# Eight PSUM banks as one ring in a linear-attention and mixture-of-experts kernel, in place of four kinds of tiles with two banks each

## The chip, the cores and the metric

The kernel runs on one core of one Trainium2 chip. The metric is the device time of one execution in microseconds (us); the median of three runs is given.

## The reference

Three blocks follow each other. A gated linear attention over 4 sequences of 768 tokens, 8 heads of 48; a gated feed-forward layer of 3072 tokens; and a mixture of 8 experts in which each token goes to the best two by noisy logits.

```python
state = alpha[:, :, t, :, None] * state + einsum('bhd,bhe->bhde', k[:, :, t], v[:, :, t])
y[:, :, t] = einsum('bhd,bhde->bhe', q[:, :, t], state)
...
x = ((x @ w1) * (x @ w2) @ w3) @ w_out          # 384 -> 1024 -> 1024 -> 384
...
noisy = x @ w_gate + log1p(exp(x @ w_noise)) * noise
# top 2 of 8 experts a token, softmax over the two
out[mask] += weight * (relu(x[mask] @ w1[e]) @ w2[e])   # 384 -> 1024 -> 384
```

## The kernel before

The work has two parts that overlap in time on the chip. The first part works through 8 groups of 384 tokens (3 chunks of 128 each). For a group, `prep_decay` and `prep_qk` turn alpha, q and k to feature-major with TensorE transposes in `to_dmajor` (L207) and scale them with scans and products on VectorE (L223, L225, L234). For each chunk j, `scores` makes the 128x128 products of k and q (L287) that VectorE masks (L294, L304), `ktok` turns k back (L316), `mix` makes the output from the state and the scores (L326, L337) and `state` updates the state (L356). `xturn` (L389) turns the output to feature-major in float16, in a high and a low part. Then comes the feed-forward layer. `wide` (L510 to L531) multiplies 384 tokens with one block of 128 columns of w1 or w2 in nine matmuls (L519 to L521); ScalarE copies the bank out (L523, tile ab), VectorE multiplies the two results (L527), ScalarE rounds to float16 (gh, L179) and VectorE makes the rest (gl, L181). `narrow` (L533 to L551) multiplies 128 tokens with the product of w3 and w_out, which the kernel makes itself once (`fuse_out_turn`, `fuse_out`, `fuse_turn`, `fuse_mul`, L457 to L493). A `narrow` has two halves of 12 matmuls on one bank; the second half needs the gl of the last `wide` blocks. `route` and `rank` choose the experts.

The second part goes through the experts: `turn` (L882) turns gathered tokens, `layer1` (L889 to L891) and `layer2` (L899 to L901) or `layer2t` (L913 to L915) multiply them, and `put` adds them to the output by indirect DMA.

The order of the work on TensorE is written out by hand. `att_units` gives the attention's units with costs, `mix_units` those of the feed-forward layer, and the loop at L1150 to L1170 takes units of the second list as long as their cost stays in a fixed relation to the attention's. TensorE runs them in just this order. The other engines' order, all waits and the tiles' places are set when the program is built, from the same code. `warm` (L1135) issues matmuls that nobody reads.

PSUM has eight banks of 128 x 512 float32 each. One pool, `ps` (L128), holds four kinds of tiles by name, with two banks each. A tile takes the bank of the tile before the last of its own kind, and its first matmul waits until that one's last reader is done.

| kind | taken by |
|---|---|
| tr | `to_dmajor`, `ktok`, `xturn`, `fuse_out_turn`, `fuse_turn`, `over_all`, `turn`, the end of `last_few` |
| sc | `scores` (two at a time), `layer1` for odd blocks |
| yu | `mix`, `state`, `scales_of`, `rank`, `layer2`, `layer2t`, `overflow_plan` |
| mm | `wide`, `narrow`, `fuse_out`, `fuse_mul`, `warm`, `layer1` for even blocks |

The program takes 738 of these tiles in all, the loop for overflowing tokens at the end included, which has no turn with this input. Most of them are written and read before the next one is taken. A bank of `narrow` or `fuse_mul` is held over both halves, with up to six others taken in between.

Of the kernel before, what the change touches and what calls it, by code (L numbers as in the profile page):

```python
# [8 lines left out]
F32 = mybir.dt.float32  # L9
# [11 lines left out]
P = 128  # L21
# [3 lines left out]
E = 8  # L25
# [37 lines left out]
T1 = 2  # L63
PGL = range(4)
NPC = 4
WE = 16
LAG = 3
WPOS = (14, 17, 17, 17, 17, 18, 18, 19, 20, 20, 20, 20)
# [15 lines left out]
def body(ctx, tc, q, k, v, alpha, mw1, mw2, mw3, mwo, wg, wn, noise, ew1, ew2, out, dbg=None):  # L84
# [40 lines left out]
    xp = ph1.enter_context(tc.tile_pool(name="xp", bufs=3))  # L125
    sp = ph1.enter_context(tc.tile_pool(name="sp", bufs=2))
    gp = ph1.enter_context(tc.tile_pool(name="gp", bufs=2))
    ps = ph1.enter_context(tc.tile_pool(name="ps1", bufs=2, space=PSUM))  # L128
    stg_ = ExitStack()
    stg = stg_.enter_context(tc.tile_pool(name="stg", bufs=2))  # L130

# [53 lines left out]
    def load(st):  # L185
# [11 lines left out]
        for c in range(TG):  # L197
# [3 lines left out]
            if st == 0:  # L201
                fetch(sum(w < len(loads) + c + 1 for w in WPOS), nc.sync)

    def to_dmajor(i, pr):
        tr = ps.tile([P, 3, P], F32, name="tr")
        for r in range(3):
            nc.tensor.transpose(tr[:, r, :], pads[i][:, r, 2 * pr:2 * pr + 2, :].rearrange("p h d -> p (h d)"),  # L207
                                ident)
        return tr
# [47 lines left out]
    def scales_of(st):  # L257

        if "ss" not in ST[st]:
            return  # L260
        V = nc.vector
        pm = ps.tile([P, 5], F32, name="yu")
        nc.tensor.matmul(pm, ones, ST[st].pop("ss"), start=True, stop=True)
        t = late.tile([P, 6], F32, name="sg")
        ti = t.bitcast(I32)
        SCL[st] = r = xp.tile([P, 4], F32, name="scl")
        V.tensor_copy(t[:, :2], pm[:, :2])
        V.tensor_reduce(t[:, 2:3], pm[:, 2:], AX.X, OP.add)
        V.tensor_scalar(ti[:, :3], ti[:, :3], 1, 0x7F800000, op0=OP.logical_shift_right, op1=OP.bitwise_and)
        V.tensor_scalar(ti[:, 3:], ti[:, :3], -1.0, float(192 << 23), op0=OP.mult, op1=OP.add)  # L270
        V.tensor_scalar(t[:, 3:], t[:, 3:], 2.0 ** 30, None, op0=OP.min)
        V.scalar_tensor_tensor(r[:, 0:1], t[:, 3:4], 2.0 ** 10, t[:, 4:5], op0=OP.mult, op1=OP.mult)
        V.tensor_scalar(r[:, 1:2], t[:, 5:6], 2.0 ** 12, None, op0=OP.mult)
        V.tensor_tensor(r[:, 2:3], r[:, 0:1], r[:, 1:2], OP.mult)
        V.tensor_scalar(r.bitcast(I32)[:, 3:4], r.bitcast(I32)[:, 2:3], -1.0, float(254 << 23), op0=OP.mult, op1=OP.add)
        CSL[st] = late.tile([P, P], F32, name="csl")
        V.tensor_scalar(CSL[st], causal, r[:, 0:1], None, op0=OP.mult)
# [3 lines left out]

    def scores(j):
        r, cols = cut(j)
        scs = [ps.tile([P, NP, P], F32, name="sc") for _ in range(2)]
        for h in range(H):
            rows = slice(64 * (h % 2), 64 * (h % 2) + D)
            nc.tensor.matmul(scs[h % 2][:, h // 2, :], r["Kt"][rows, h // 2, cols], r["Qt"][rows, h // 2, cols],  # L287
                             start=True, stop=True)
        SM[j] = []
        for s in range(2):  # L290
            if j // TG in SCL:
                sf = late.tile([P, NP, P], F32, name="sf")
                sm = late.tile([P, 2, NP, P], F16, name="sm16", bufs=4)
                nc.vector.tensor_tensor(sf, scs[s], CSL[j // TG][:, None, :].to_broadcast([P, NP, P]), OP.mult)  # L294
                split(sf, sm[:, 0], sm[:, 1], engine=nc.gpsimd)
                SM[j].append(sm)
                continue
            sm = ap_.tile([P, NP, P], F32, name="sm", bufs=3)
            if j in AFF:
                nc.scalar.activation(sm, scs[s], AF.Copy)  # L300
                nc.gpsimd.affine_select(out=sm, in_=sm, pattern=[[0, NP], [1, P]], compare_op=OP.is_ge, fill=0.0,
                                        base=0, channel_multiplier=-1)
            else:
                nc.vector.tensor_tensor(sm, scs[s], causal[:, None, :].to_broadcast([P, NP, P]), OP.mult)  # L304
            SM[j].append(sm)
        if j // TG in SCL:
            VH[j] = late.tile([P, 2, H, D], F16, name="vh")
            split(VT[j], VH[j][:, 0], VH[j][:, 1], SCL[j // TG][:, 1:2])

    def ktok(j):  # L310
        if j % NC == NC - 1:
            return
        r, cols = cut(j)
        kt = ps.tile([P, NP, P], F32, name="tr")
        for pr in range(NP):
            nc.tensor.transpose(kt[:, pr, :], r["Kt"][:, pr, cols], ident)  # L316
        KS[j] = ap_.tile([P, NP, P], F32, name="ks")
        nc.scalar.activation(KS[j], kt, AF.Copy)

    def mix(j):  # L320
        r, cols = cut(j)
        y = ps.tile([P, NP, 2 * D], F32, name="yu")
        n = 0
        if j % NC:
            for pr in range(NP):
# [22 lines left out]
    def state(j):  # L348
# [2 lines left out]
        if c == NC - 1:  # L351
            return
        ks, vt = KS.pop(j), VT[j]
        u = ps.tile([P, NP, 2 * D], F32, name="yu")
        for pr in range(NP):
            nc.tensor.matmul(u[:112, pr, :], ks[:, pr, :112], vt[:, 2 * pr:2 * pr + 2, :], start=True, stop=True)  # L356
        Z, Zn = Zs[j % 2], Zs[(j + 1) % 2]
# [25 lines left out]
    def xturn(j):  # L383
        ys = YS.pop(j)
        if j % TG == 0:
            XT[j // TG] = xp.tile([P, 2 * NK, G], F16, name="xT")
        xt = ps.tile([P, 2 * NK, P], F16, name="tr")
        for kk in range(2 * NK):
            nc.tensor.transpose(xt[:, kk, :], ys[:, kk // NK, kk % NK * P:(kk % NK + 1) * P], ident16)  # L389
        nc.scalar.activation(XT[j // TG][:, :, j % TG * P:(j % TG + 1) * P], xt, AF.Copy)  # L390
# [65 lines left out]

    def fuse_out_turn(f):  # L457
        wo = FS.pop(f)
        tr = ps.tile([P, NK, P], F32, name="tr")
        for kk in range(NK):  # L460
            nc.tensor.transpose(tr[:, kk, :], wo[:, kk * P:(kk + 1) * P], ident)
        FO[f] = stg.tile([P, NK, P], F32, name="woT")
        nc.scalar.activation(FO[f], tr, AF.Copy)

    def fuse_out(f):
        woT = FO.pop(f)
        pr = ps.tile([P, 2 * E], F32, name="mm")
        for kk in range(NK):
            nc.tensor.matmul(pr, woT[:, kk, :], wr[:, kk, :], start=kk == 0, stop=kk == NK - 1)
        split(pr, woh[:, f, DM:], wol[:, f, DM:], SW)  # L470

    def fuse_turn(f, hf):
        s = FS.pop((f, hf))
        th = stg.tile([P, 4, P], F16, name="w3h", bufs=3)
        tl = stg.tile([P, 4, P], F16, name="w3l", bufs=3)
        tr = ps.tile([P, 4, P], F32, name="tr")
        for j in range(4):
            nc.tensor.transpose(tr[:, j, :], s[:, j * P:(j + 1) * P], ident)
        split(tr, th, tl, SW)
        FT[f, hf] = (th, tl)  # L480

    def fuse_mul(f, hf):
        th, tl = FT.pop((f, hf))
        if hf == 0:
            FT[f] = ps.tile([P, W], F32, name="mm")
        pw = FT[f]
        for j in range(4):
            kk = 4 * hf + j
# [21 lines left out]
    def wide(g, f, i, c1=G):  # L510
# [3 lines left out]
        c0 = GS.get((g, f, i), 0)  # L514
        GS[g, f, i] = c1
        cs, n = slice(c0, c1), c1 - c0
        pm = ps.tile([P, G], F32, name="mm")[:, :n]
        for kk in range(NK):
            nc.tensor.matmul(pm, wab[i][0][:, kk, fs], xT[:, kk, cs], start=kk == 0, stop=False)  # L519
            nc.tensor.matmul(pm, wab[i][0][:, kk, fs], xT[:, NK + kk, cs], start=False, stop=False)  # L520
# [12 lines left out]
    def narrow(g, t, part):  # L533
        ts = slice(t * P, (t + 1) * P)
        if part == 0:
            X2[g, t] = ps.tile([P, W], F32, name="mm")
            if t == 0:
                X2[g] = sp.tile([P, TG, W], F32, name="x2", bufs=1)
                X2[g, "sq"] = sp.tile([P, 5, TG], F32, name="am")
# [98 lines left out]
    def rank(g):  # L638
# [1 line left out]
        V = nc.vector  # L640
        sh = [P, TG, E]
        M, oh, rr, md = RT.pop(g)
        pk = ps.tile([P, TG, E], F32, name="yu")
        nc.tensor.matmul(pk, before, M[:, 0], start=True, stop=False)
        nc.tensor.matmul(pk, ones, M[:, 1], start=False, stop=True)
        rk = sp.tile(sh, F32, name="rk")
# [1 line left out]
        if g == NG - 2:  # L648
            rb = sp.tile([P, E], BF, name="rb")
            V.tensor_copy(rb, R)  # L650
            pt = ps.tile([P, E], F32, name="yu")
            nc.tensor.matmul(pt, ones, rb, start=True, stop=True)
            V.tensor_scalar(skip, pt[:, :NFR], -1.0, float(G0), op0=OP.mult, op1=OP.add)
            V.tensor_scalar(skip, skip, 0.0, None, op0=OP.max)
# [174 lines left out]
    def weight_steps(src, e, n, m, hi, lo, sc):  # L829
# [19 lines left out]

        def over_all():  # L850

            s["pm"] = ps.tile([P, 1], F32, name="tr")
            nc.tensor.matmul(s["pm"], part, s["m"], start=True, stop=True)

        def scales():
# [21 lines left out]
        return xg  # L877

    def turn(xg, xT, t):
        pt = ps.tile([P, 2 * NK, P], F16, name="tr")  # L880
        for j in range(2 * NK):
            nc.tensor.transpose(pt[:, j, :], xg[:, j * P:(j + 1) * P], ident16)  # L882
        nc.scalar.activation(xT[:, :, t * P:(t + 1) * P], pt, AF.Copy)  # L883

    def layer1(f, w1h, w1l, xT, n, hh, hl):
        fs = slice(f * P, (f + 1) * P)
        pm = ps.tile([P, n], F32, name=("mm", "sc")[f % 2])
        for kk in range(NK):
            nc.tensor.matmul(pm, w1h[:, kk, fs], xT[:, kk, :n], start=kk == 0, stop=False)  # L889
            nc.tensor.matmul(pm, w1h[:, kk, fs], xT[:, NK + kk, :n], start=False, stop=False)  # L890
# [3 lines left out]

    def layer2(w2h, w2l, hh, hl, c0, n, mt, wv, t, midway=None):
        ts = slice(c0, c0 + n)
        py = ps.tile([P, DM], F32, name="yu")
        for f in range(NF):
            nc.tensor.matmul(py[:n], hh[:, f, ts], w2h[:, f], start=f == 0, stop=False)  # L899
            nc.tensor.matmul(py[:n], hh[:, f, ts], w2l[:, f], start=False, stop=False)  # L900
# [5 lines left out]
    def layer2t(w2h, w2l, hh, hl, c0, n):  # L906

        ts = slice(c0, c0 + n)
        py = ps.tile([P, NK, n], F32, name="yu")
        for k in range(NK):  # L910
            ks = slice(k * P, (k + 1) * P)
            for f in range(NF):
# [55 lines left out]
    def last_few(e):  # L968
# [3 lines left out]
        yt = layer2t(EW[e][3], EW[e][4], *EH[e, 1], t * P, n)  # L972

        def rest():
            pt = ps.tile([P, NK, P], F32, name="tr")
            for k in range(NK):
                nc.tensor.transpose(pt[:n, k, :], yt[:, k, :], ident)
            put(pt[:n].rearrange("p k d -> p (k d)"), n, mt, WV[e, 1], t)
# [100 lines left out]
    def overflow_plan():  # L1079
# [1 line left out]
        V = nc.vector  # L1081
        rb = ep.tile([P, E], BF, name="rb", bufs=1)
        V.tensor_copy(rb, R)
        pc = ps.tile([P, E], F32, name="yu")
        nc.tensor.matmul(pc, ones, rb, start=True, stop=True)
        c = ep.tile([1, 4, E], F32, name="oc", bufs=1)
        ci = c.bitcast(I32)
# [46 lines left out]

    def warm(n):  # L1135

        pm = ps.tile([P, HF], F32, name="mm") if n else None
        for _ in range(n):
            nc.tensor.matmul(pm, ident16, idle, start=True, stop=True)

# [68 lines left out]
```

## Time and profile before

| | us |
|---|---|
| three runs | 1043.92, 1041.92, 1037.54 |
| median | 1041.92 |
| the profiled execution | 1039.59 |
| its span, first to last instruction | 1037.7 |
| TensorE busy in it | 949.7 (92%) |
| VectorE, ScalarE, GpSimd busy | 617.2, 503.9, 252.4 |
| mean granted TensorE clock | 0.974 |

The engines are PE (TensorE matmul), PEld (TensorE weight load), DVE (VectorE), ACT (ScalarE), POOL (GpSimd) and SP (SyncE). L519 is line 519 of the kernel. A tile is named by the variable that holds it, without its number; names that share a place can stand for each other. Matmuls are pipelined: one is recorded with its whole passage, longer than the distance from its start to the next one's start.

### The profile page before, as it was taken

The numbers are of one execution on the slowest core, as the hardware profiler recorded it, in microseconds if no ns is written. First come the engines' busy times: TensorE is split into PE (matmuls) and PEld (weight loads), VectorE is DVE, ScalarE is ACT, GpSimd is POOL, SyncE is SP. The second block draws the span as 40 slices with busy tenths as digits, with TensorE's granted clock in tenths as the row PEclk, the third lists the DMA queues.
The fourth block names the chain that finished last, engine by engine and source line by source line (L and its number), as shares of the span: only waits on it lengthen the run. The fifth ranks groups of instructions, "written<-read, shape, count | busy, mean of one in ns | idle before, by whom it ended". The sixth has DMA issues, their size and how long they took to land.

```text
span 1037.7 us, 18277 instructions
## 1 busy us (share of the span) xinstructions
PE 949.7 (92%) x7159; PEld 624.1 (60%) x7159; DVE 617.2 (59%) x1696; ACT 503.9 (49%) x972; POOL 252.4 (24%) x246
## 2 busy tenths in 40 slices
PE   7879999999989888989898889999999999999993
PEld 4667767776656555666655444765656565656562
DVE  6796777576869586686736647626363544445210
ACT  3856665353645645545444444435353544444320
POOL 2111110040211303031304134233242424232212
PEclk9889899999999999999999999999999999999997
DMA  9876571337405024000301336345443444543212
GB/s 250 207 137 100 142 194 49 72 66 200 85 17 91 10 61 55 23 2 16 100 24 33 113 77 167 92 95 160 90 128 91 111 115 89 137 89 76 28 16 36
DMA packets 144472, 94.58 MB, mean 91 GB/s; under 512 B 112112, under 2 KB 130112, under 8 KB 144384
## 3 DMA queue, kind: packets, MB, share of 16 engines
q1 hardware_dynamic: 127824, 57.02, 23.1%
q0 software_dynamic: 16560, 36.37, 15.8%
q8 instruction: 57, 0.93, 0.4%
q14 instruction: 31, 0.25, 0.1%
HBM read 73.06 MB, written 20.31 MB: 90 GB/s over the span
## 4 chain that ended last, share of the span: by engine, by line
PE 63%; DVE 20%; ACT 7%; issue 6%; DMA 3%; another core or an unknown queue 0%; POOL 0%; POOLq 0%; DVEq 0%; SPq 0%; ACTq 0%
PE yu L901 5%; PE yu L899 5%; PE yu L900 5%; PE sc L890 3%; PE sc L891 3%; PE sc L889 3%; PE mm L891 3%; PE mm L890 3%; PE mm L889 3%; PE mm L521 3%; PE mm L519 3%; PE mm L543 3%; PE mm L545 3%; PE mm L544 2%; PE mm L520 2%
## 5 line engine op out<-in xcount | busy, mean ns | idle before, releaser
L923 POOL DMA_INDIRECT out_dram<-ysb,mt x56 | 89.7, 1602 | 264.9 <-ACT ysb L922 127.1
L900 PE MATMUL yu<-el,hh 128*128 128x384 f16 x384 | 125.8, 328 | 2.5 <-DVE el L183 2.5
L899 PE MATMUL yu<-eh,hh 128*128 128x384 f16 x384 | 126.0, 328 | 0.0
L901 PE MATMUL yu<-eh,hl 128*128 128x384 f16 x384 | 125.9, 328 | 0.0
L183 DVE SCALAR_TENSOR_TENSOR el<-es,esc,eh 128x512 f16<-128x512 f32 (+1 forms) x80 | 66.8, 856 | 52.3 <-ACT eh L179 50.6
L922 ACT ACTIVATE ysb<-yu,wv 128x384 f32<-128x384 f32 x48 | 27.9, 581 | 129.5 <-PE yu L901 68.0
L673 POOL DMA_INDIRECT table<-md,ad x48 | 47.8, 996 | 156.8 <-DVE ad L670 78.3
L523 ACT ACTIVATE ab<-mm 128x384 f32<-128x384 f32 (+2 forms) x136 | 62.7, 467 | 46.6 <-PE mm L521 38.9
L893 DVE SCALAR_TENSOR_TENSOR hl<-mm,hh 128x512 f16<-128x512 f32 (+1 forms) x64 | 37.6, 587 | 78.2 <-ACT hh L892 78.2
L519 PE MATMUL mm<-xT,w1h 128*128 128x384 f16 (+2 forms) x204 | 66.9, 329 | 12.4 <-ACT ab L523 12.3
L519 PE MATMUL mm<-xT,w0h 128*128 128x384 f16 (+2 forms) x204 | 65.1, 320 | 12.7 <-ACT ab L523 11.7
L181 POOL TENSOR_TENSOR sm<-sf,sm 128x512 f16<-128x512 f32 x24 | 28.1, 1190 | 170.4 <-ACT sm L179 170.4
L891 PE MATMUL mm<-xT,el 128*128 128x512 f16 (+1 forms) x192 | 65.1, 339 | 4.3 <-DVE el L183 4.3
L874 POOL DMA_INDIRECT xg<-x2s,mt x56 | 54.8, 978 | 53.7 <-PE mm L891 13.3
L520 PE MATMUL mm<-xT,w1h 128*128 128x384 f16 (+2 forms) x204 | 66.9, 329 | 0.0
L521 PE MATMUL mm<-xT,w1l 128*128 128x384 f16 (+2 forms) x204 | 66.8, 329 | 0.0
L889 PE MATMUL mm<-xT,eh 128*128 128x512 f16 (+1 forms) x192 | 65.1, 339 | 1.0 <-ACT xT L883 1.0
L890 PE MATMUL sc<-xT,eh 128*128 128x512 f16 (+1 forms) x192 | 65.9, 343 | 0.0
L891 PE MATMUL sc<-xT,el 128*128 128x512 f16 (+1 forms) x192 | 65.8, 343 | 0.0
L889 PE MATMUL sc<-xT,eh 128*128 128x512 f16 (+1 forms) x192 | 65.7, 342 | 0.0
L543 PE MATMUL mm<-Wh,gh 128*128 128x400 f16 x192 | 63.9, 333 | 1.9 <-ACT ab L523 1.7
L890 PE MATMUL mm<-xT,eh 128*128 128x512 f16 (+1 forms) x192 | 65.1, 339 | 0.0
(294 smaller groups left out, 2405.9 us busy)
## 6 DMA issues: line engine op xcount, KB each, us to landing
es<-in_moe_w_dram SPq DMA_DIRECT2D x32, 768.0 KB
s<-in_moe_w_dram POOLq DMA_DIRECT2D x16, 512.0 KB
out_dram<-zero POOLq DMA_DIRECT2D x5, 960.0 KB
v<-in_v_dram SPq DMA_DIRECT2D x24, 192.0 KB
x2s<-xr SPq DMA_DIRECT2D x24, 192.0 KB
pad<-in_alpha_dram SPq DMA_DIRECT2D x21, 192.0 KB
pad<-in_q_dram SPq DMA_DIRECT2D x21, 192.0 KB
pad<-in_k_dram SPq DMA_DIRECT2D x21, 192.0 KB
```

The lines of the kernel that those rows point to most:

```text
L183: nc.vector.scalar_tensor_tensor(lo, src, scale, hi, op0=OP.mult, op1=OP.subtract)
L519: nc.tensor.matmul(pm, wab[i][0][:, kk, fs], xT[:, kk, cs], start=kk == 0, stop=False)
L520: nc.tensor.matmul(pm, wab[i][0][:, kk, fs], xT[:, NK + kk, cs], start=False, stop=False)
L521: nc.tensor.matmul(pm, wab[i][1][:, kk, fs], xT[:, kk, cs], start=False, stop=kk == NK - 1)
L543: nc.tensor.matmul(pm, gh[:, ts], Wf[0][:, f], start=f == 0, stop=False)
L889: nc.tensor.matmul(pm, w1h[:, kk, fs], xT[:, kk, :n], start=kk == 0, stop=False)
L890: nc.tensor.matmul(pm, w1h[:, kk, fs], xT[:, NK + kk, :n], start=False, stop=False)
L891: nc.tensor.matmul(pm, w1l[:, kk, fs], xT[:, kk, :n], start=False, stop=kk == NK - 1)
L899: nc.tensor.matmul(py[:n], hh[:, f, ts], w2h[:, f], start=f == 0, stop=False)
L900: nc.tensor.matmul(py[:n], hh[:, f, ts], w2l[:, f], start=False, stop=False)
L901: nc.tensor.matmul(py[:n], hl[:, f, ts], w2h[:, f], start=False, stop=f == NF - 1)
L923: nc.gpsimd.indirect_dma_start(out=out, out_offset=bass.IndirectOffsetOnAxis(ap=mt[:n, t, 0:1].bitcast(U32), axis=0), in_=ys[:n], in_offse ...
```

## The change

All tiles of the pool take their bank from one ring. The pool has eight buffers of one name, and a helper `bank` gives a view of the needed shape. A tile's first matmul then waits for the last reader of the tile that was taken eight tiles before it, of whatever kind. All 23 places that take a PSUM tile are changed in the same way; five of them stand here.

```diff
+PB = 512
...
-    ps = ph1.enter_context(tc.tile_pool(name="ps1", bufs=2, space=PSUM))
+    ps = ph1.enter_context(tc.tile_pool(name="ps1", bufs=8, space=PSUM))
...
+    def bank(*shape, dt=F32):
+
+        t = ps.tile([P, PB], F32, name="ps")
+        if dt != F32:
+            t = t.bitcast(dt)
+        n = 1
+        for x in shape:
+            n *= x
+        t = t[:, :n]
+        return t if len(shape) == 1 else t.rearrange("p (a b) -> p a b", a=shape[0])
+
     def to_dmajor(i, pr):
-        tr = ps.tile([P, 3, P], F32, name="tr")
+        tr = bank(3, P)
...
-        scs = [ps.tile([P, NP, P], F32, name="sc") for _ in range(2)]
+        scs = [bank(NP, P) for _ in range(2)]
...
-        y = ps.tile([P, NP, 2 * D], F32, name="yu")
+        y = bank(NP, 2 * D)
...
-        pm = ps.tile([P, G], F32, name="mm")[:, :n]
+        pm = bank(n)
...
-        pm = ps.tile([P, n], F32, name=("mm", "sc")[f % 2])
+        pm = bank(n)
```

## Rows read from the trace of the kernel before

**Rows 1.** Stretches: start:end, length, busy us by engine, granted clock, DMA share, GB/s.
```profile
8.50:24.50 16.00, 11.20 (x72) 6.36 (x71) 15.60 (x38) 4.49 (x6) 0.00 (x0) 1.00 1.07 306
50.00:130.00 80.00, 68.90 (x502) 54.61 (x500) 63.10 (x157) 49.38 (x97) 11.38 (x18) 0.86 0.66 129
130.00:525.00 395.00, 360.79 (x2850) 250.23 (x2849) 284.31 (x936) 207.65 (x447) 74.59 (x75) 1.00 0.30 68
...
640.00:1000.00 360.00, 359.95 (x2775) 224.63 (x2774) 167.99 (x307) 161.60 (x276) 113.01 (x88) 1.00 0.41 97
```

**Rows 2.** TensorE's waits, 130 to 525 us: total us, times, longest us.
```profile
PE mm L519 <- ACT ab L523: 19.6, 16, 3.5
PE tr L207 <- DVE Qt L234: 4.8, 6, 1.5
PE tr L389 <- DVE Qt L234: 2.0, 4, 0.9
PE mm L543 <- ACT ab L523: 1.7, 2, 0.9
PE tr L478 <- DVE Qt L234: 1.1, 1, 1.1
PE tr L207 <- DVE w3l L183: 0.9, 2, 0.7
...
PE tr L389 <- DVE Kt L234: 0.7, 1, 0.7
PE mm L545 <- DVE gl L181: 0.6, 1, 0.6
PE tr L316 <- DVE Qt L234: 0.5, 1, 0.5
```

**Rows 3.** Timeline of TensorE around 345 us (start, us, instruction, idle time before).
```profile
341.55 0.33 PE L520 MATMUL mm<-xT,w0h 128*128 128x384 f16 x1
341.72 0.33 PE L521 MATMUL mm<-xT,w0l 128*128 128x384 f16 x1
345.55 0.48 PE L519 MATMUL mm<-xT,w1h 128*128 128x384 f16 x1 [3.50 <-ACT ab L523]
...
346.14 0.52 PE L521 MATMUL mm<-xT,w1l 128*128 128x384 f16 x1
346.46 0.52 PE L519 MATMUL mm<-xT,w1h 128*128 128x384 f16 x1
```

**Rows 4.** Timeline of ScalarE before that start.
```profile
334.05 0.47 ACT L523 ACTIVATE ab<-mm 128x384 f32<-128x384 f32 x1
...
343.48 0.49 ACT L344 ACTIVATE ys<-yu 128x384 f16<-128x384 f32 x1 [2.62 <-PE mm L521]
...
345.01 0.48 ACT L523 ACTIVATE ab<-mm 128x384 f32<-128x384 f32 x1
```

**Rows 5.** TensorE's waits, 50 to 130 us.
```profile
PE tr L207 <- DVE Qt L234: 2.2, 1, 2.2
...
PE mm L519 <- ACT ab L523: 1.9, 2, 1.7
PE tr L207 <- DVE Kt L234: 1.3, 1, 1.3
```

**Rows 6.** Timeline of TensorE and VectorE at the end of a `wide` run.
```profile
520.97 0.32 PE L519 MATMUL mm<-xT,w0h 128*128 128x384 f16 x1 [3.23 <-ACT ab L523]
...
525.77 0.56 DVE L181 TENSOR_TENSOR gl<-ab,gh 128x384 f16<-128x384 f32 x1 [0.59 <-ACT gh L179]
...
528.12 0.33 PE L545 MATMUL mm<-Wh,gl 128*128 128x400 f16 x1
```

**Rows 7.** Timeline of VectorE and TensorE around 96 us.
```profile
95.76 1.03 PE L326 MATMUL yu<-Zs,Qt 112*128 112x96 f32 x8
...
98.63 0.67 DVE L304 TENSOR_TENSOR sm<-sc,causal 128x512 f32<-128x512 f32 x1
```

**Rows 8.** TensorE's waits, 525 to 640 us.
```profile
PE mm L891 <- DVE el L183: 4.3, 1, 4.3
```

More of the change, by code (lines that the diff above doesn't have):

```diff
@@ L261, in scales_of @@
         V = nc.vector
-        pm = ps.tile([P, 5], F32, name="yu")
+        pm = bank(5)
         nc.tensor.matmul(pm, ones, ST[st].pop("ss"), start=True, stop=True)
@@ L313, in ktok @@
         r, cols = cut(j)
-        kt = ps.tile([P, NP, P], F32, name="tr")
+        kt = bank(NP, P)
         for pr in range(NP):
@@ L353, in state @@
         ks, vt = KS.pop(j), VT[j]
-        u = ps.tile([P, NP, 2 * D], F32, name="yu")
+        u = bank(NP, 2 * D)
         for pr in range(NP):
@@ L386, in xturn @@
             XT[j // TG] = xp.tile([P, 2 * NK, G], F16, name="xT")
-        xt = ps.tile([P, 2 * NK, P], F16, name="tr")
+        xt = bank(2 * NK, P, dt=F16)
         for kk in range(2 * NK):
@@ L458, in fuse_out_turn @@
         wo = FS.pop(f)
-        tr = ps.tile([P, NK, P], F32, name="tr")
+        tr = bank(NK, P)
         for kk in range(NK):
@@ L466, in fuse_out @@
         woT = FO.pop(f)
-        pr = ps.tile([P, 2 * E], F32, name="mm")
+        pr = bank(2 * E)
         for kk in range(NK):
@@ L475, in fuse_turn @@
         tl = stg.tile([P, 4, P], F16, name="w3l", bufs=3)
-        tr = ps.tile([P, 4, P], F32, name="tr")
+        tr = bank(4, P)
         for j in range(4):
@@ L484, in fuse_mul @@
         if hf == 0:
-            FT[f] = ps.tile([P, W], F32, name="mm")
+            FT[f] = bank(W)
         pw = FT[f]
@@ L535, in narrow @@
         if part == 0:
-            X2[g, t] = ps.tile([P, W], F32, name="mm")
+            X2[g, t] = bank(W)
             if t == 0:
@@ L642, in rank @@
         M, oh, rr, md = RT.pop(g)
-        pk = ps.tile([P, TG, E], F32, name="yu")
+        pk = bank(TG, E)
         nc.tensor.matmul(pk, before, M[:, 0], start=True, stop=False)
@@ L650, in rank @@
             V.tensor_copy(rb, R)
-            pt = ps.tile([P, E], F32, name="yu")
+            pt = bank(E)
             nc.tensor.matmul(pt, ones, rb, start=True, stop=True)
@@ L850, in over_all @@
         def over_all():
-            s["pm"] = ps.tile([P, 1], F32, name="tr")
+            s["pm"] = bank(1)
             nc.tensor.matmul(s["pm"], part, s["m"], start=True, stop=True)
@@ L879, in turn @@
     def turn(xg, xT, t):
-        pt = ps.tile([P, 2 * NK, P], F16, name="tr")
+        pt = bank(2 * NK, P, dt=F16)
         for j in range(2 * NK):
@@ L896, in layer2 @@
         ts = slice(c0, c0 + n)
-        py = ps.tile([P, DM], F32, name="yu")
+        py = bank(DM)
         for f in range(NF):
@@ L908, in layer2t @@
         ts = slice(c0, c0 + n)
-        py = ps.tile([P, NK, n], F32, name="yu")
+        py = bank(NK, n)
         for k in range(NK):
@@ L974, in rest @@
         def rest():
-            pt = ps.tile([P, NK, P], F32, name="tr")
+            pt = bank(NK, P)
             for k in range(NK):
@@ L1083, in overflow_plan @@
         V.tensor_copy(rb, R)
-        pc = ps.tile([P, E], F32, name="yu")
+        pc = bank(E)
         nc.tensor.matmul(pc, ones, rb, start=True, stop=True)
@@ L1135, in warm @@
     def warm(n):
-        pm = ps.tile([P, HF], F32, name="mm") if n else None
+        pm = bank(HF) if n else None
         for _ in range(n):
```

## The prediction

> **What bounds the kernel now.** I read the busy shares, the stretches, the engine's own waits, then single instructions around them. TensorE is busy 92% of the span, but the share mixes two regimes. From 640 to 1000 us it is busy 359.95 of 360 us at a full granted clock [rows 1]: the expert stage is bound by the matmuls themselves. From 130 to 525 us it is busy 360.79 of 395, at a clock of 1.00, while VectorE has 284 busy and ScalarE 208. So this stretch is TensorE's too, but with 34 us of idle time that could go. From 50 to 130 the clock averages 0.86 and VectorE is busy 79% [rows 1].
>
> The waits of TensorE say what that idle time is [rows 2]. The first line, 19.6 us in 16 waits, is a first matmul of `wide` (L519) released by the ScalarE copy that empties an earlier `wide` bank (L523). This is no data: L519 reads only xT and weights. It is the second-last bank of the kind "mm" that was not empty. The next lines are the same for the kind "tr": transposes (L207, L389, L478, L316) whose inputs are long there, released by the VectorE product (L234) or split that reads an older transpose. The longest case shows it [rows 3, 4]. The matmuls of a `wide` unit start 0.16 to 0.17 apart, its last at 341.72; the next unit starts only at 345.55, which is 0.06 after ScalarE's copy of 345.01 + 0.48 = 345.49 ended. ScalarE had stood for 2.62 us and then did other work. Meanwhile the two "sc" and two "yu" banks did not help, since a kind has only its own two.
>
> **The change, part by part.** No instruction is added or removed: the same matmuls, reads and DMAs, in the same order on TensorE, which the kernel writes out by hand. What changes is which earlier reader a unit waits for: the reader of the tile eight units back, of any kind, in place of two back of its own kind.
>
> *What it removes.* From 130 to 525 the bank waits are the lines of [rows 2] but the one on gl: 19.6 + 4.8 + 2.0 + 1.7 + 1.1 + 0.9 + 0.7 + 0.5 = 31.3 us in 33 waits. Each also costs a refill: a matmul is recorded as 0.33 long but starts 0.16 after the one before [rows 3], so an idle time counted from the recorded end hides another 0.17. 33 x 0.17 = 5.6, in all 36.9. In the case at 345.55 the bank of the unit eight back (an earlier `wide`) was emptied at 334.05 + 0.47 = 334.52 [rows 4], eleven us before. I counted units back through the written order in the same way at each of these waits: the eighth-last bank was free at least 3 us before the wait ended, every time.
>
> That wait also let the clock fall: the nine matmuls after 345.55 start 0.32 apart instead of 0.16 [rows 3], the lower of the two levels (1.2 GHz), before the step is 0.16 again. 9 x 0.16 = 1.4 us, which go with it.
>
> From 50 to 130 the three clear bank lines are 2.2 + 1.9 + 1.3 = 5.4 us, 4 waits, with refills 6.1 [rows 5]. From 8.5 to 24.5 us there are short waits too, but VectorE is busy 15.60 of 16 us there [rows 1] and its decay scans set the pace, so I count nothing (bounds 0 and about 3). After 640 there is nothing to win.
>
> *What comes late next.* A unit that starts early meets its data. Data waits of 130 to 525 are small now: `narrow` on gl 0.6 is the longest line of them [rows 2]. The bank waits are spread over many places, the others' total work fits (VectorE 284 us of 395 would be 284 of 370, 77%), and eight banks are some ten us of TensorE's work (313 units in 395 us, 1.26 each) against single lags of up to 3.5. But a lag does not vanish: it is passed on until ScalarE and VectorE have caught up, and each run of `wide` ends in a `narrow` that needs the last gl. At 520.97, after a wait of 3.23, that gl ended at 525.77 + 0.56 = 526.33, and the matmul of `narrow` that reads it starts at 528.12 [rows 6]: only 1.8 us in hand. Bounds: everything returns (36.9), or only what the data leave in hand. Of the two long waits, the one at 345.55 has no `narrow` for 9 us and should go whole, the one at 520.97 at least 1.8 of 3.2. The sum of both is 5.3 of 6.7, 79%; for the small ones in denser places I take less, and two thirds overall: 24.6. For 50 to 130, where VectorE is the fuller engine and converts weights, a third of 6.1: 2.0 (bounds 0 and 6.1).
>
> *What it adds.* One late reader now stops every kind. `scores` at 84.82 leaves a bank that VectorE reads only at 98.63 to 99.30, and eight units on a `mix` starts at 95.76 [rows 7]: under the ring it would wait 3.54 us, and behind it in TensorE's queue stand `fuse_out` and the next `wide`. I find four such places in the whole trace, 3.54, 1.66, 1.16 and 1.11, sum 7.5 us. Some will move with the rest, so I take half, 3.7 (bounds: 0, and more than 7.5 if TensorE, now earlier, meets more of them).
>
> *Transition and end.* Of the waits from 525 to 640 the longest, 4.3 us on el (L891), is for expert weights [rows 8]; those stay, and bank waits are under 1 us there. The expert weights are asked for by a position in the program, not by a time, so the stretch should move forward as a whole. The part behind 1000 us is output DMA. Both zero.
>
> **Sum.** 24.6 + 2.0 + 1.4 - 3.7 = 24.3 us. The profiled execution took 1039.59 (span 1037.7), so 1015.3; the median of the three runs shown is 2.3 above it, so 1017.6, rounded 1018.
>
> **A rule that speaks against it.** The Trainium skill, "TensorE: Matmul & The Clock Gate", section "A second HAM failure mode: psum-queue depth-cycling", tells of a kernel that cycled through the PSUM banks each iteration and whose TensorE paused between groups so that its clock went up and down. Here the trace has groups going round banks all the time (two per kind) at 1.00 from 130 to 525 [rows 1], and the one place where I see the clock fall follows a 3.50 us wait that the ring removes. By the rule the ring would cost, by the trace it gives 1.4 back. That is the last rival below.
>
> **The rivals.**
> 1. *The waits become data waits.* ScalarE is behind because it stands in its own queue waiting for VectorE; the ring moves neither. For it: `narrow` on gl has 1.8 us in hand after 520.97. Against: the longest line of data waits now is 0.6 us [rows 2]. If a third of 36.9 returns and nothing between 50 and 130: 12.3 + 1.4 - 3.7 = 10.0, so 1032.
> 2. *All of it returns* and late banks disappear, since VectorE's order, made at build time, follows TensorE's earlier times: 36.9 + 6.1 + 1.4 = 44.4, so 997.
> 3. *The ring is none.* If the planner gave a unit the bank freed last instead of the oldest, the waits would stay. For it: nothing in the trace; against: TensorE starts 0.06 after the second-last of its kind. 1042.
> 4. *Slower: a late bank stops all.* `scores` and `mix` banks are read late on purpose, when VectorE comes to them. If TensorE, running ahead, reached them in each of the 24 chunks, at 2 us per chunk: 48 us against 28.0 won, so 20 slower, 1062. It decides from 1.2 us per chunk (28.0 / 24); the trace of before has 7.5 / 24 = 0.3.
> 5. *Slower: the clock goes up and down* while units go round the ring. With 0.86 as from 50 to 130 [rows 1] in place of 1.00, 395 x 0.14 = 55 us lost against 24 won: about 1073.
>
> **How the numbers follow.** What a measurement of this kernel tells from no change is about 1%, 10.4 us, so below 1031.5 is faster. Forecast 0.65 (its own range 1006 to 1030); rival 1 0.15; rival 2 0.10; rival 3 0.04; rival 4 0.04; rival 5 0.02. Faster: 0.64 of the forecast, 0.07 of rival 1, 0.10 of rival 2, together 0.81. Within 1%: 0.01 + 0.08 + 0.04 = 0.13. Slower: 0.06. The range from 1000 to 1034 leaves out rivals 3 to 5 (0.10), most of rival 2 (0.08) and a little of the rest: about 0.2.
>
> **What would show it.** Right: the line L519 <- ACT L523 falls from 19.6 to under 5 us, the L207, L389, L478 lines <- DVE L234 nearly vanish, TensorE's idle time from 130 to its last `wide` falls by some 20 us, the stretch of experts lasts as long as before, and the slow step after 345 is gone. Some us appear as `narrow` on gl or as waits of any kind on L304 or L294 (a `scores` bank). Wrong: L519 waits as long, now on L523 of eight back or on L304; or `narrow` and `mix` wait over 15 us; or the expert stage is longer, which no step here allows.

## The result, and the profile after

The changed kernel takes 1013.79 us (median of four runs, 1010.66 to 1015.12), the kernel before on the same chip 1040.96 (1037.54 to 1043.92). The ratio is 0.9736, 95% interval [0.9697, 0.9774]: 27 us faster, 4 below the 1018 forecast and well inside the range. The total was right. Two of its terms were not: one was some 6 us too high, the other 7 too low, so that the total comes out this near is luck.

The profiled execution took 1014.1 us, its span is 1012.2. In the lines below, a line of the changed kernel is the old number plus 12 (L519 is L531, L523 is L535, L294 is L306), and every PSUM tile is called `ps`. The stretches, to be read against [rows 1]:

```profile
8.50:24.50 16.00, 10.77 (x66) 6.54 (x65) 14.76 (x36) 4.53 (x7) 0.48 (x1) 0.94 1.07 307
50.00:130.00 80.00, 74.31 (x577) 59.90 (x576) 70.86 (x172) 55.10 (x110) 12.78 (x22) 0.89 0.71 144
130.00:500.00 370.00, 352.21 (x2787) 247.17 (x2786) 274.41 (x924) 198.77 (x438) 73.62 (x73) 0.98 0.31 69
...
620.00:980.00 360.00, 360.00 (x2774) 224.47 (x2772) 163.33 (x296) 158.37 (x271) 114.45 (x86) 1.00 0.41 95
```

The experts run as before, 360.00 of 360 busy. From 50 to 130 TensorE is busy 74.31 instead of 68.90. From 130 on it is busy 95% of the stretch instead of 91%, but the granted clock is 0.98 and no longer 1.00. What TensorE waits for from 130 to 525 us (total, times, longest), against [rows 2]:

```profile
PE ps L657 <- DVE M L646: 5.1, 4, 2.0
PE ps L338 <- DVE Zs L393: 2.6, 1, 2.6
PE ps L656 <- DVE M L644: 2.2, 2, 2.0
PE ps L299 <- DVE Kt L246: 2.0, 2, 1.3
PE ps L349 <- issue: 1.9, 3, 0.8
PE ps L531 <- DVE Zs L392: 1.5, 1, 1.5
...
PE ps L555 <- ACT gh L180: 0.9, 2, 0.7
...
PE ps L557 <- DVE gl L182: 0.6, 1, 0.6
```

The line that led before, `wide` on ScalarE's copy, 19.6 us, is gone, and so are the transposes on L246 (L234 before). What leads now is data: `rank` (L656, L657) multiplies the mask M that `route` makes, 7.3 us in six waits; `mix` (L338) waits for the state Zs; `scores` (L299) for Kt. One clear bank wait is left, 1.5 us: L531 reads no Zs, yet it starts when VectorE's L392 is done, which reads the bank of `state` to make Zs.

From 50 to 130, against [rows 5], the two transposes on a bank are gone too:

```profile
PE ps L338 <- DVE Zs L380: 1.7, 1, 1.7
PE ps L299 <- DVE Kt L246: 1.5, 2, 1.1
PE ps L299 <- DVE Qt L246: 1.0, 1, 1.0
```

And from 500 to 620 the wait for the expert weights stands much as it was in [rows 8], 4.8 us after 4.3:

```profile
PE ps L903 <- DVE el L184: 4.8, 1, 4.8
```

**Where the time went.** TensorE runs the same units in the same order, so the start of a unit in one trace can be set against its start in the other. The gain is -0.4 at the unit that starts at 51 us in the trace of before, 8.7 at 132, 11.1 at 202, 24.8 at 528, 25.4 at 585 and 25.6 at 1017. In lengths of the same pieces of work: 81.4 became 72.4 (51 to 132 us of before), 69.8 became 67.4 (to 202), 326.2 became 312.5 (to 528), 488.6 became 487.8 (the rest). The first of these is the surprise in size: 9 us came from a piece for which the prediction had 2. The two profiled executions are 25.5 us apart, the medians 27.

### The profile page after: what moved, and what is told of

Read it like the earlier page. It is cut to its first block, busy times and chain, and to the rows that moved or that the text cites. A ratio compares the mean times of both kernels' runs of the same rounds, so it can differ in the third digit from the quotient of the medians.

```text
span 1012.2 us, 18282 instructions
## 1 busy us (share of the span) xinstructions
PE 947.1 (94%) x7159; PEld 628.9 (62%) x7159; DVE 613.5 (61%) x1696; ACT 498.9 (49%) x972; POOL 254.0 (25%) x246
## 5 line engine op out<-in xcount | busy, mean ns | idle before, releaser
L905 DVE SCALAR_TENSOR_TENSOR hl<-ps,hh 128x512 f16<-128x512 f32 (+1 forms) x128 | 74.5, 587 | 105.1 <-ACT hh L904 99.8
L903 PE MATMUL ps<-xT,el 128*128 128x320 f16 (+1 forms) x384 | 130.9, 341 | 4.8 <-DVE el L184 4.8
L901 PE MATMUL ps<-xT,eh 128*128 128x320 f16 (+1 forms) x384 | 130.7, 340 | 1.3 <-ACT xT L895 1.3
L902 PE MATMUL ps<-xT,eh 128*128 128x320 f16 (+1 forms) x384 | 130.7, 340 | 0.0
L912 PE MATMUL ps<-el,hh 128*128 128x384 f16 x384 | 125.9, 328 | 2.5 <-DVE el L184 2.5
L913 PE MATMUL ps<-eh,hl 128*128 128x384 f16 x384 | 125.8, 328 | 0.0
L911 PE MATMUL ps<-eh,hh 128*128 128x384 f16 x384 | 125.8, 328 | 0.0
L535 ACT ACTIVATE ab<-ps 128x384 f32<-128x384 f32 (+2 forms) x136 | 61.4, 465 | 34.3 <-PE ps L533 23.3
L531 PE MATMUL ps<-xT,w0h 128*128 128x384 f16 (+2 forms) x204 | 67.2, 331 | 2.6 <-DVE Zs L392 1.5
L533 PE MATMUL ps<-xT,w0l 128*128 128x384 f16 (+2 forms) x204 | 67.0, 330 | 1.1 <-issue 1.1
L532 PE MATMUL ps<-xT,w0h 128*128 128x384 f16 (+2 forms) x204 | 67.3, 331 | 0.0
L531 PE MATMUL ps<-xT,w1h 128*128 128x384 f16 (+2 forms) x204 | 66.5, 326 | 0.0
L532 PE MATMUL ps<-xT,w1h 128*128 128x384 f16 (+2 forms) x204 | 66.4, 326 | 0.0
L533 PE MATMUL ps<-xT,w1l 128*128 128x384 f16 (+2 forms) x204 | 66.2, 325 | 0.0
```

Of the source, the lines that this page charges most:

```text
L533: nc.tensor.matmul(pm, wab[i][1][:, kk, fs], xT[:, kk, cs], start=False, stop=kk == NK - 1)
L903: nc.tensor.matmul(pm, w1l[:, kk, fs], xT[:, kk, :n], start=False, stop=kk == NK - 1)
L905: nc.vector.scalar_tensor_tensor(hl[:, f], pm, 0.0, hh[:, f], op0=OP.max, op1=OP.subtract)
L913: nc.tensor.matmul(py[:n], hl[:, f, ts], w2h[:, f], start=False, stop=f == NF - 1)
```

## The experiments

The chip of the pair above is called A here, that of eight of the experiments B (whether A and B are one chip is not known), that of the first four C. The kernel before took 1041 us on A, 1037 on B, and 1021.5 on C. That last number was not expected and became the main question. The expectations of the first four were written from the times of chip A, so only their differences can be set against what C measured.

**Which kinds matter (chip C).** Four runs: two partial rings, and a ring in one part of the time only. `bank` gets the kind as an argument for that.

```diff
-    def bank(*shape, dt=F32):
-
-        t = ps.tile([P, PB], F32, name="ps")
+    def bank(kind, *shape, dt=F32):
+
+        name, bufs = {'mm': ('ms', 4), 'sc': ('ms', 4), 'tr': ('tr', 2), 'yu': ('yu', 2)}[kind]
+        t = ps.tile([P, PB], F32, name=name, bufs=bufs)
```

> The kinds mm and sc share one ring of four banks; tr and yu keep two each. Theory (each bank wait removed is worth its own time, wherever it lies): the waits of wide (19.6 us from 130 to 525, 1.7 of narrow, 2.2 earlier, with refills some 27 us) go and those of tr stay; at the six tenths that the whole ring got of its waits this is 15 us, so about 1026. Rival one (wide is all that counts): the whole gain, 1014. Rival two (a freed kind only shows the wait of the next): under 6 us, above 1035.

In b_tr4 it is the transposes that share four banks with "sc" (the edit against a_mm4):

```diff
-        name, bufs = {'mm': ('ms', 4), 'sc': ('ms', 4), 'tr': ('tr', 2), 'yu': ('yu', 2)}[kind]
+        name, bufs = {'mm': ('mm', 2), 'sc': ('ts', 4), 'tr': ('ts', 4), 'yu': ('yu', 2)}[kind]
```

> The kinds tr and sc share one ring of four banks; mm and yu keep two each. Theory: the waits of the transposes (10 us from 130 to 525, some 6 earlier, with refills 20) go and those of wide stay; six tenths are 12 us, so about 1029. Rival one (wide is all that counts): no gain, 1041. Rival two (a freed kind only shows the wait of the next): under 6 us, above 1035.

Measured: a_mm4 1015.2 us (ratio 0.9944, [0.9912, 0.9976]), b_tr4 1013.95 (0.9934, [0.9908, 0.996]); the kernel before 1021.54 on this chip. Either pair of banks that `wide` or the transposes get beyond their own two brings 6 to 8 us here; the expectations had 15 and 12. The waits from 130 to 525 of a_mm4:

```profile
PE tr L220 <- DVE Qt L247: 4.8, 6, 1.5
PE tr L402 <- DVE Qt L247: 3.5, 4, 1.8
PE tr L329 <- DVE Qt L247: 3.4, 2, 2.4
```

and of b_tr4:

```profile
PE mm L532 <- ACT ab L536: 11.2, 11, 2.4
PE ts L300 <- DVE Qt L247: 2.8, 2, 2.0
```

Each partial ring clears nearly all waits of the kinds in it and leaves those of the others: the transposes keep their 4.8 on L220 and wait longer than before on L402 and L329, `wide` keeps 11.2. (There is no trace of the kernel before on C; on A `wide` had 19.6, and f_early below has 10.5 on C.) So the waits are the banks', as the prediction read them, and are not those of one reader.

The second pair switches at the end of the own fused weights, at about 188 us: f_early has the ring up to there and then the four kinds, g_late the reverse.

```diff
     def end_of_weights():
-        nonlocal late
+        nonlocal late, ps, ring
         stg_.close()
+        psx.close()
+        ps = ph1.enter_context(tc.tile_pool(name="ps2", bufs=8, space=PSUM))
+        ring = False
```

> The ring of eight until the weights of the feed-forward layer are made (the pool is closed and opened again there), then the four kinds with two banks each. Theory (the ring's lead of 11 us at that unit against the kernel before is real and stays): about 1030. The step of my forecast (2 us before 130 and a share of the rest up to there): 1036. Rival (an early lead is used up later, since the later units then wait for data): 1041 or close to it.

> The other half: four kinds until the weights are made, then the ring of eight. Theory (the two halves add up to 27): about 1026. The step of my forecast (nearly all of the gain is here): 1020. Rival (the late half would give more without the early lead): under 1020, so that the halves add up to over 31 us.

Measured: f_early 1014.22 (0.9928, [0.9905, 0.9951]), 7.3 us below the kernel before; g_late 1018.29 (0.9968, [0.9949, 0.9988]), 3.2 below; expected were some 11 and 15. On this chip the early part brought more than the late one, and both together only some 10.5: too little for the 27 of chip A. Either the parts did not add up, or the late gain was smaller on this chip.

**The pair again, on chip B.** Both kernels unchanged, and two variants of the ring.

> The kernel before itself, unchanged, with a profile: the runs of it beside the first four experiments took 1021.5 us where the first four had taken 1041. Theory (the chip or the time of the run sets something that stands on the path in the kernel before): about 1021 again on the same chip, the profile shows the 14 us between the units around 262 and 610 us gone, and idle times of ScalarE and VectorE that no instruction explains are shorter than before. Rival (the experiments' form of the program is what is faster): 1041.

> The changed kernel itself, beside the kernel before on the same chip. Theory (bank waits removed are worth what they were in the first comparison): 27 us under the kernel before, so about 994 if that takes 1021. Rival (the ring only hid a disturbance of the first chip, and where that is gone its worth is that of the early part): 1010 to 1014, 7 to 11 us under the kernel before.

Measured: z_before 1036.95 us (ratio 1.0, [0.998, 1.0021]), z_after 1012.34 (0.9779, [0.9742, 0.9816]), 25 us apart. The result holds in a second measurement. The expectation of 1021 for z_before was meant for chip C and could not be tested on B. So C is the odd one; as it was used at one time only, the chip and the occasion can't be told apart.

**Scores with banks of their own.** If a late `scores` bank stops the ring, two banks of their own for `scores` and a ring of six for the rest should win that back.

```diff
+        name, bufs = {'mm': ('ps', 6), 'yu': ('ps', 6), 'tr': ('ps', 6), 'sc': ('sc', 2)}[kind]
+        t = ps.tile([P, PB], F32, name=name, bufs=bufs)
```

> The scores keep two banks of their own, all else has a ring of six. Theory (a late reader of a scores bank stops every kind; such places sum to some 7 to 9 us): 3 to 6 us under the changed kernel, if six banks are still enough. Rival (six banks are too few, since a unit held over both halves is followed by up to six others): 2 to 8 us over it.

Measured: 1014.36 us (0.9796, [0.9752, 0.9841]), beside 1012.34 for z_after: 2 us more, which this measurement does not tell from none. Its waits from 130 to 525:

```profile
PE ps L658 <- DVE M L647: 4.4, 3, 2.0
...
PE ps L556 <- ACT gh L180: 2.2, 2, 1.6
PE ps L657 <- ACT ab L536: 2.1, 1, 2.1
...
PE ps L532 <- ACT ab L536: 0.7, 2, 0.5
```

With six banks some of the old waits on L536 come back. The 3 to 6 us that were expected from `scores` are not there. What its own two banks win and what the smaller ring loses are not separated here; together they come to nothing that shows.

**Rank later.** The longest data wait of the ring is `rank` on the mask M. The experiment moves `rank` from behind `wide` block 3 of a group to behind block 5 (but not for the last group, on which the experts wait).

```diff
-                if f == RF and g:
+                if f == (RF if g == NG - 1 else 5) and g:
```

> The changed kernel with rank two blocks of wide later (after block 5 instead of 3, but for the last group). In the changed kernel TensorE waits 7.3 us in six places for the route's mask M at rank. Theory (these waits are a bound of their own): they go, 4 to 7 us under the changed kernel. Rival (rank is only where TensorE meets VectorE again, and the next unit that needs VectorE waits instead): within 2 us of the changed kernel.

Measured: 1006.91 us (1003.19 to 1008.67; ratio 0.971, [0.967, 0.975]), 5.4 below z_after on the same chip, and the best of all kernels here. From 130 to 525 us:

```profile
PE ps L299 <- DVE Kt L246: 5.2, 5, 2.0
PE ps L557 <- DVE gl L182: 2.2, 1, 2.2
...
PE ps L657 <- DVE M L646: 1.0, 1, 1.0
```

The waits for M fall from 7.3 to 1.0; a part of that turns up at L299 and L557, the next data in line. The 5.4 us lie within the 4 to 7 expected. So these data waits in the ring are real time, and what they cost the ring could be had back by the order of the work.

**What differs between the chips.** The longest wait of before ends at 345.55 [rows 3], and [rows 4] shows ScalarE idle for 2.62 us ahead of it. The prediction took that idle time as ScalarE's being behind. The trace of the kernel before holds more; here the matmuls of `mix` whose result ScalarE reads at 343.48, and what GpSimd does at the time (and around the second long wait, 520.97):

```profile
336.23 0.98 POOL L673 DMA_INDIRECT table<-md,ad  x1 [17.50 <-DVE ad L670]
...
337.52 1.04 POOL L673 DMA_INDIRECT table<-md,ad  x1 [0.30 <-issue]
...
338.35 0.77 PE L337 MATMUL yu<-vh,sm 128*128 128x48 f16 x24
...
342.65 0.96 POOL L673 DMA_INDIRECT table<-md,ad  x1 [0.30 <-issue]
...
510.14 1.05 POOL L673 DMA_INDIRECT table<-md,ad  x1 [6.45 <-DVE ad L670]
...
516.69 0.96 POOL L673 DMA_INDIRECT table<-md,ad  x1 [0.30 <-issue]
```

`mix` is done at 338.35 + 0.77 = 339.12, but its completion event is recorded at 343.46, and ScalarE's read follows at 343.48. ScalarE was not busy elsewhere: it was told 4.3 us late. (The view puts this wait down to L521; but the tile read is the yu of `mix`, and the events come in the order of the work.) Over the same time GpSimd issues six scatters in a row (L673), which `rank` makes for each group. I counted, over the trace, TensorE's completions whose next recorded event comes more than 1 us after the recorded end, between 230 and 530 us:

| kernel, chip | late completions | longest, us |
|---|---|---|
| before, A | 16 | 4.9 |
| before (z_before), B | 12 | 4.2 |
| ring (z2_after, below), B | 8 | 3.6 |
| a_mm4, b_tr4, f_early, g_late, C | 0 | - |

The ring on A (after) has 13 by the same count. On A and B some events have no record (the trace of before has 825 for 840 completions), and the next one then stands for them, so these counts may be a few too high; on C none is missing. On A and B nearly all of the late ones fall within a burst of scatters or less than 2 us after it. On C the same bursts run, and nothing is late. At the same place of the work, f_early on C (the four kinds by then):

```profile
322.23 0.98 POOL L688 DMA_INDIRECT table<-md,ad  x1 [17.51 <-DVE ad L685]
...
324.36 0.77 PE L352 MATMUL yu<-vh,sm 128*128 128x48 f16 x24
...
326.76 0.48 ACT L359 ACTIVATE ys<-yu 128x384 f16<-128x384 f32 x1
...
328.64 0.96 POOL L688 DMA_INDIRECT table<-md,ad  x1 [0.30 <-issue]
```

Here `mix` ends at 325.13, and ScalarE, coming from other work, reads at 326.76 without idle time. The same program on chip B (f2_early, below) ends this `mix` at 329.49, and ScalarE reads it 4.1 us later, after idle time:

```profile
333.59 0.49 ACT L359 ACTIVATE ys<-yu 128x384 f16<-128x384 f32 x1 [2.52 <-PE mm L536]
```

**The test of the bursts (chip B).** Four kernels in one go: the ring, f_early again, and both kernels of the pair with the scatters of six groups left out.

```diff
-        for j in range(2):
+        for j in (range(2) if g in (0, NG - 1) else ()):
             for t in range(TG):
                 i = nc.gpsimd.indirect_dma_start(
```

> The ring itself, unchanged, beside the kernel before on this chip. The kernel before has taken 1037 to 1041 us on two chips and 1021.5 on a third; the ring 1012 to 1014 on two. Theory A (the ring makes the time independent of late completions that some chips have and others have not): 1009 to 1014 here, whatever the kernel before takes. Theory B (a chip is simply slower or faster for every kernel): the ring keeps its ratio of 0.974 to 0.978, so 994 to 999 if the kernel before takes 1021 here. If the kernel before takes 1037 to 1041, both give 1010 to 1016 and this run only anchors the others.

> The ring up to the end of the own fused weights (about 188 us), then the four kinds with two banks each, now beside the whole ring on one chip. If the late part of the work gains as the trace of the ring says (some 15 us after 188 us on a chip where the kernel before takes 1037 to 1041): 1026 to 1029 here, 13 to 16 above the ring. If the late gain is small on this chip (the kernel before at 1021): 1012 to 1016, 2 to 5 above the ring. If the four kinds cost nothing late: within 2 us of the ring.

> The kernel before, with the scatter of the groups 1 to 6 into the table of the experts left out (the six indirect DMAs that GpSimd issues in a row after each rank; the experts then work on other tokens, the same number of blocks). In the trace of before, completions of TensorE come up to 4.9 us late inside five of these bursts, and the longest bank waits (345.55, 520.97) follow two of them. Theory A (the burst itself holds up the engines' completions): the two waits of over 3 us vanish, and the time falls by 6 to 16 us against the kernel before on this chip (less if this chip shows no late completions to begin with). Theory B (the bursts only fall together with something else): within 3 us of the kernel before, and the late completions stay at the same places in the order of the work.

> The ring with the same scatters left out. Theory A (bursts hold up completions, and the ring already takes most of that up): 0 to 6 us below the ring, so the distance from the kernel before with the same scatters left out shrinks from some 25 to 10 to 18. Theory B (the bursts are innocent): the ring's own time within 2 us, distance to the kernel before as it was.

Measured, the kernel before at 1036.97 us (16 runs, 1032.44 to 1040.46):

| kernel | us | ratio, interval |
|---|---|---|
| z2_after | 1013.54 | 0.9777 [0.9734, 0.982] |
| f2_early | 1029.74 | 0.9934 [0.9916, 0.9952] |
| n_before | 1028.5 | 0.9925 [0.9898, 0.9953] |
| n_after | 1012.28 | 0.9762 [0.9724, 0.98] |

Without those bursts the kernel before is 8.5 us faster, the ring 1.3; the distance between them falls from 23.4 to 16.2. n_before and n_after lie where theory A had them. z2_after could not tell the theories apart on this chip, and f2_early lies 0.7 above the first of its ranges. In n_before the late completions between 230 and 530 us are gone, all of them.

There is a control within the same run. At 531.72 GpSimd issues seven gathers in a row (L874, the tokens of an expert), which the experiment left in. `wide` ends a unit there at 537.16 + 0.33 = 537.49, its event is recorded at 539.56, and ScalarE waits for it:

```profile
536.81 0.94 POOL L874 DMA_INDIRECT xg<-x2s,mt  x1 [0.30 <-issue]
537.16 0.33 PE L521 MATMUL mm<-xT,w0l 128*128 128x384 f16 x1
538.06 0.97 POOL L874 DMA_INDIRECT xg<-x2s,mt  x1 [0.30 <-issue]
539.64 0.49 ACT L523 ACTIVATE ab<-mm 128x384 f32<-128x384 f32 x1 [2.22 <-PE mm L521]
```

So bursts of gathers come with late events too, and not the scatters alone. n_after has five late completions by the same count, all of them in its burst of gathers.

The place of the longest wait in n_before:

```profile
335.18 0.77 PE L337 MATMUL yu<-vh,sm 128*128 128x48 f16 x24
...
338.65 0.48 ACT L344 ACTIVATE ys<-yu 128x384 f16<-128x384 f32 x1
...
340.70 0.32 PE L519 MATMUL mm<-xT,w1h 128*128 128x384 f16 x1 [1.42 <-ACT ab L523]
```

ScalarE reads without idle time, and the bank wait that follows is 1.42 us in place of 3.50. Its waits from 130 to 525:

```profile
PE mm L519 <- ACT ab L523: 9.2, 10, 2.3
PE tr L207 <- DVE Qt L234: 4.8, 6, 1.5
PE tr L389 <- DVE Qt L234: 1.4, 2, 0.9
```

On the same chip, with the bursts (z_before):

```profile
PE mm L519 <- ACT ab L523: 14.7, 11, 3.4
```

So of the 14.7 us of `wide` on L523, 5.5 came with the bursts; the waits of the transposes on L207 did not. (The 19.6 were on A.) f2_early, 1029.74, lies 16.2 above the ring on B, where f_early on C took 1014.22: the same program, 15.5 us apart on two chips, with the four kinds in its late part. Of the 12.9 us between the two profiled executions, 9.0 lie in that part. The late part, from 202 to 528 us of before, in lengths of the same work:

| | four kinds | ring | gain |
|---|---|---|---|
| A | 326.2 (before) | 312.5 (after) | 13.7 |
| B | 323.2 (z_before) | 309.5 (z2_after) | 13.7 |
| B, no bursts there | 311.9 (n_before) | 304.6 (n_after) | 7.3 |
| C | 314.2 (f_early) | 307.0 (g_late) | 7.2 |

Each length is from one profiled execution, but the two lower rows agree: without late completions, whether because the bursts are left out or because the chip has none, the ring gains 7 us in this part. With them it gains 14.

These gains do not all reach the whole time. The ring itself became 4.9 us shorter in the late part without the bursts (309.5 to 304.6), but only 1.3 in all: the work behind it, where the experts have other tokens, took 2.3 us longer. On C the work behind the late part took g_late 3.4 us longer than f_early, which fits with g_late being only 3.2 below the kernel before.

Leaving the scatters out also frees GpSimd, which is another way to gain time. It can't be most of it, as far as two chips can be compared: f_early on C has the same bursts on GpSimd and no late event, and its late part is 9.0 us shorter than that of z_before and only 2.3 longer than that of n_before.

Some things stay open. The experiment left out the scatters' issue on GpSimd and their writes together, so it does not say which of them holds the events up. Why chip C shows none was not found. And n_before, at 1028.5, is still 7 us above the kernel before on C; bursts of indirect DMAs that were kept may be a part of that, which no run shows. The whole ring was not run on C; if f_early and g_late add up, it would take some 1011 there (an estimate from 1021.5 - 7.3 - 3.2).

## Why the prediction was right, and where it was not

*The bound and the bank waits: right.* The step said that TensorE waits for banks, not for data. The L523 line went from 19.6 us to nothing, the L234 lines too, the expert stage kept its length, and the partial rings clear just the kinds in them.

*Two thirds of 36.9 and a clock term, less 3.7, from 130 on (22.3 together): too high.* The work from 132 to 528 us of before became 2.4 + 13.7 = 16.1 us shorter. Idle time there fell by 1.3 + 15.1 = 16.4. So of the 36.9 us, 20.8 did not make the work shorter; the prediction had 14.6 (12.3 + 3.7 - 1.4). Of the 20.8, 14.9 is idle time that came back (31.3 - 16.4), and 5.9 is what refills and the clock were to give: busy time did not fall. What came back as idle time is for the most part data waits, which is rival 1 in part: 7.3 on M, 2.6 on Zs, 2.0 on Kt. The step looked for the data in hand at `narrow` (gl), which waits 0.6 as before; it did not ask what `rank` needs, which had been covered by the bank waits ahead of it, all but 0.3 us. Where the prediction did look, it was right; it looked at one consumer.

*Clock: wrong in sign.* The slow step after 345.55 did go. But the new data waits let the clock fall elsewhere. In the trace after, stretches of 6 and 5 us:

```profile
424.00:430.00 6.00, 3.60 (x13) 1.75 (x14) 5.24 (x24) 2.84 (x8) 1.47 (x2) 0.61 0.00 0
...
485.00:490.00 5.00, 2.60 (x24) 1.84 (x22) 4.13 (x15) 3.03 (x7) 2.27 (x3) 1.00 0.01 0
490.00:495.00 5.00, 4.85 (x43) 3.96 (x44) 1.12 (x3) 0.52 (x1) 3.72 (x4) 0.66 0.50 158
```

and the single matmuls in them:

```profile
424.43 0.19 PE L656 MATMUL ps<-M,before 128*128 128x24 bf16 x1 [1.97 <-DVE M L644]
426.59 0.18 PE L657 MATMUL ps<-M,ones 128*128 128x24 bf16 x1 [1.97 <-DVE M L646]
...
487.10 0.50 PE L401 MATMUL ps<-ident,ys 128*128 128x128 f16 x6
490.15 2.00 PE L338 MATMUL ps<-Zs,Qt 112*128 112x96 f32 x8 [2.56 <-DVE Zs L393]
```

Two waits of 1.97 us close together, and one of 2.56, each with a mean granted clock near 0.6 beside it; the eight matmuls of L338 take 2.00 us instead of the 1.03 of [rows 7]. The stretch from 130 to 500 has 0.98 where it had 1.00; on B it is 0.98 in z_after and z2_after against 0.99 in z_before.

*Head-of-line cost, 3.7: too high.* One bank wait of 1.5 us is clear in the trace. Taking `scores` out of the ring gained nothing, but that run also made the ring smaller.

*2.0 from 50 to 130: far too low.* The work from 51 to 132 us became 9.0 us shorter on A; on B 8.5 (z_before against z_after) and 4.9 (against z2_after), each from one execution, and the two of the ring are the same kernel. On A 5.4 of it is idle time, about all of the 6.1 that the step bounded it by, and 3.6 is time in which TensorE was busy. The step took a third, since VectorE was at 79% there; VectorE went to 89% and followed. Where the 3.6 came from is not shown. The granted clock from 50 to 130 was 0.86 before and 0.89 after on A, but 0.89 in z_before and 0.89 and 0.87 in z_after and z2_after, so that it does not rise with the ring every time.

*The rivals.* Rival 2 (all returns) holds for 50 to 130 on A and not behind it. Rival 3 fell with the first run. Rival 4, a late bank in each chunk, has one such place. Rival 5: the Trainium skill, "TensorE: Matmul & The Clock Gate", section "A second HAM failure mode: psum-queue depth-cycling", tells of a kernel that goes round the banks, with short pauses between its groups from which its clock oscillates. The trace has 0.98 over 370 us of going round all eight, and the falls shown above follow waits for data. It agrees in that the clock fell behind pauses; that going round the banks makes the pauses does not show here.

*The cause of the longest waits: not seen.* The prediction explained 3.50 us by ScalarE's being behind, from the row that shows it idle for 2.62. Its idle time was the effect of a completion that came late. The number for what goes with the ring was none the worse, since the bank eight back was free either way. But it could not tell that a part of the gain hangs on the late events: on chip C, where there are none, the two halves of the ring together gave 10.5 us in place of 24.

## What to carry to other kernels

Banks that are split by kind let one late reader stop TensorE while others stand empty; a ring of all of them showed one clear wait of its own here, 1.5 us, and takes up lags of several us. When such waits go, look at every consumer's data behind them, not at the one that waits now: here a move of `rank` by two blocks was worth another 5 us. And where a wait is long, follow it back until an engine was really busy; if it was idle too, look for what held its event up.

## What the runs showed of the hardware

Bursts of six indirect scatters from GpSimd, some 7.5 us long, came with completion events of TensorE up to 4.9 us late on chips A and B and none over 1 us late on C. Bursts of gathers did the same (2.1 us in n_before). With the scatters of six groups left out, a kernel that waits on its second-last bank became 8.5 us faster, a kernel with a ring 1.3. The same program took 1021.5 us on C and 1037 to 1041 on B and A, where the ring took 1012 to 1014. So how much the change is worth differs between chips, or between the times at which they were used: 23 to 27 us there, and by the estimate above some 10 on C.
